# A forgetting-attention and FFN kernel on one core: q and k loaded per pair of heads and copied across partitions by ScalarE and VectorE

## The chip, the cores and the metric

The kernel runs on one core of a Trainium2 chip. The metric is the time of one execution on the device in microseconds; lower is better. Besides its memories a core has TensorE (PE; its weight loads are the rows PEld), VectorE (DVE), ScalarE (ACT), GpSimd (POOL) and SyncE (SP), which in this kernel issues all DMA transfers. Each engine works through its own queue in order; an instruction that waits holds up everything behind it on that engine.

## What is computed

```
scores = q k^T / 8 ;  cum = cumsum(log(clip(f, 1e-4, 1)))
scores = where(causal, -1e9, scores + cum[i] - cum[j])
attn   = softmax(scores)                     # 8 batches, 8 heads, S = 576, D = 64
x      = (attn v), heads side by side        # 4608 tokens x 512
h      = x w_in ; g = max(0.01 h, h) ; out = g w_out      # 512 -> 2048 -> 512, float32
```

## The kernel before, in words

Everything that needs full accuracy is split into a high part (`fp32r`, a float32 rounded for TensorE) and the low rest, and multiplied in two or three products. There are two kinds of work, and they run interleaved.

*Heads.* 64 heads, 8 to a batch, in two forms: in batches 0, 1 and 2 the first 256 queries are done in early steps ahead of the loop, so that only queries from 256 on are left there (24 heads, 320 columns of q); the other 40 heads are whole (576 columns). For head `t` the loop at L639 holds four kinds of step:

- `load(t)` (L215): q and k of one head come into `qraw` and `kraw`. Each is 64 rows (D) by 576, and each is loaded twice, into the lower and the upper 64 partitions (L223, four transfers). Both tiles have a single buffer. For the first head of a pair it also fetches v of both heads into `vm` (L227, L228).
- `split(t)` (L327): makes the operands of two products of 128 rows. The first is `s1` by `m1`: `m1` is the high part of k in both halves, `s1` the low part of q in the lower half and the high part in the upper half. The second is `s2` by `m2`: the upper half is the high part of q against the low part of k; in the lower half rows 0 to 3 hold the decay and ones, the others zeros. ScalarE makes the high parts (L337, L338, 128 partitions by 576), GpSimd the low ones by subtraction (L342, L343, through the helper at L133), and a transfer copies the high part of q from `s1` into `s2` (L339). Two small transfers bring the decay's rows (L340, L341). `s1` and `m1` have two buffers, `s2` and `m2` are four fixed tiles, a and b for even and odd heads. At last v is split into `vs` (L346, L347).
- `scores(t, i)` (L349): for each of up to five chunks of queries the two products (L362); VectorE adds the causal triangle `tri` and takes the extreme (L367); ScalarE takes the exponential and its sum (L373).
- `transposes`, `values`, `inverse`, `normalise` of the head before, `t - 1`: TensorE turns the chunks (L412), ScalarE and VectorE split the result into `ph` and `pl` (L424, L426); products with `vs` follow (L451), and ScalarE and VectorE add the two halves into `x` (L458 through the small tile `y`, L459). Once per pair `inverse` takes the reciprocals (L469, L470), turns them (`rt`, L472), writes them out (`rows`, L478) and reads them back across partitions (`rb`, `rbr`, L482); `normalise` multiplies (L494) and writes `xd` to memory (L497).

*FFN.* Groups of 256 tokens. `fetch_group` reads a group back from `xd` as `xs` (L508), `split_group` splits it (VectorE at L513, GpSimd), and the products `h` (L541) and `o` (L574) follow, with `g`, `gh`, `gl` between them (ScalarE L548, VectorE L551, GpSimd L553). A generator yields the FFN in small quanta, and `fill(step)` puts some of them between the steps of the heads, so that TensorE has something to do while the heads' chains run.

*What sets the order.* The text of the kernel gives each instruction its priority, and a planner (the scheduler of the tile framework) lays out every engine's queue from it: an instruction is put in line when, by the planner's own estimates of durations, what it needs is ready and its buffer is free. So a queue need not follow the order of the text, and work of a head can stand a step ahead of its place in the text. On the chip the queues then keep the planner's order, whatever really comes first.

Of the kernel before, what the change touches and what calls it, by code (L numbers as in the profile page):

```python
# [8 lines left out]
F32 = mybir.dt.float32  # L9
# [4 lines left out]
ALU = mybir.AluOpType  # L14

P = 128
# [21 lines left out]
def forgetting_attention_ffn(ctx, tc, qT, kT, v4, vr, f, w_in, w_out, out):  # L38
# [6 lines left out]
    nc = tc.nc  # L45
# [168 lines left out]

    def load(t):  # L215

        s, c0, c1 = tasks[t]
        h = state[t] = {}
        a, n = c0 * P, S
        for name, src, lo in (("q", qT, a), ("k", kT, 0)):  # L220
            x = h[name] = one.tile([P, S], F32, tag=f"{name}raw", name=f"{name}raw_{t}")
            for o in range(2):
                nc.sync.dma_start(x[o * D:(o + 1) * D, lo:n], src[s][:, lo:n])  # L223
        if s % 2 == 0:
            g = s // 2
            vm = fixed["vm"]
            nc.sync.dma_start(vm[:, :, :NFULL], v4[g])  # L227
            nc.sync.dma_start(vm[:REST, :, NFULL], vr[g])  # L228
            pairs[s // 2, c0] = {}
# [97 lines left out]
    def split(t):  # L327


        s, c0, c1 = tasks[t]  # L330
        h = state[t]
        a, n = c0 * P, S
        x = "ab"[t % 2]
        s1 = h["s1"] = one.tile([P, S], F32R, tag="s1", name=f"s1_{t}", bufs=2)
        m1 = h["m1"] = one.tile([P, S], F32R, tag="m1", name=f"m1_{t}", bufs=2)
        s2, m2 = h["s2"], h["m2"] = fixed["s2" + x], fixed["m2" + x]
        nc.scalar.copy(s1[:, a:n], h["q"][:, a:n])  # L337
        nc.scalar.copy(m1[:, :n], h["k"][:, :n])  # L338
        nc.sync.dma_start(s2[D:, a:n].bitcast(F32), s1[D:, a:n].bitcast(F32))  # L339
        nc.sync.dma_start(s2[2:4, a:n].bitcast(F32), dec_q[s][:, a:n])  # L340
        nc.sync.dma_start(m2[:2, :n].bitcast(F32), dec_k[s][:, :n])  # L341
        minus(s1[:D, a:n], h["q"][:D, a:n], s1[:D, a:n].bitcast(F32))  # L342
        minus(m2[D:, :n], h["k"][D:, :n], m1[D:, :n].bitcast(F32))  # L343
        o = s % 2
        vs, vm = fixed["vs"][:, o], fixed["vm"][:, o]
        nc.scalar.copy(vs[:, :, :D], vm)  # L346
        minus(vs[:, :, D:], vm, vs[:, :, :D].bitcast(F32))  # L347

    def scores(t, i):  # L349
# [9 lines left out]
        for x, (a, b) in enumerate(parts):  # L359
# [6 lines left out]
            at = TRI - P + m - n + a  # L366
# [96 lines left out]
    def inverse(t):  # L463
# [9 lines left out]
        main = one.tile([P, NFULL * P], F32, tag="part0", name=f"rb_{t}")  # L473
        rest = one.tile([P, 2 * P], F32, tag="part1", name=f"rbr_{t}")
        flat = rest[:2 * NCH, P:]
# [4 lines left out]
        for y, lo, hi in ((main[:, a:], a + P, NCH * P), (rest[:, :REST], a, a + REST)):  # L480
            for o in range(2):
                nc.sync.dma_start(  # L482
                    y[o * D:(o + 1) * D], to[o:o + 1, lo:hi].broadcast_to([D, hi - lo])
                )
        pairs[s // 2, c0]["r"] = main, rest

    def normalise(t):

        s, c0, c1 = tasks[t]
        pair = pairs[s // 2, c0]  # L490
        x, (main, rest) = pair["x"], pair["r"]
        a, n = c0 * P, S
        for y, lo, hi in ((main[:, a:], a + REST, n), (rest[:, :REST], a, a + REST)):
            nc.vector.tensor_tensor(x[:, lo:hi], x[:, lo:hi], y, op=ALU.mult)  # L494
        b, hp = s // HPB, (s % HPB) // 2
        at = place[b, a]
        nc.sync.dma_start(xd[hp * P:(hp + 1) * P, at:at + n - a], x[:, a:n])  # L497
# [117 lines left out]
    TRI = S  # L615
# [21 lines left out]
    load(0)  # L637
    split(0)
    for t in range(nt + 1):  # L639
        heads[0] = t < nt  # L640
        if t + 1 < nt:
            load(t + 1)
# [6 lines left out]
        for i in range(5):  # L649
# [4 lines left out]
            if i == 1 and t and tasks[t - 1][0] % 2:  # L654
                inverse(t - 1)
            fill(step)
# [47 lines left out]
```

## Time and profile before

| | |
|---|---|
| median of 3 runs | 1221.16 us (1220.94 to 1221.28) |
| the profiled execution | 1219.51 us |
| its span, first to last instruction | 1217.7 us |
| TensorE's mean granted clock | 0.947 |
| DMA, share of 16 engines | 29.7% |
| HBM read, written | 82.62 MB, 18.58 MB |

How to read the lines. In the list of groups a line stands for all instructions of one line of the kernel, one engine and one shape: `out<-in`, shapes, count, then busy time and mean duration in ns, then the idle time of the engine just before them and what ended it. In the view of waits a row says which engine's line waited for what: us in total, times, longest. The timeline gives start and duration in us, and in brackets the idle time before and what ended it; rows `SPq` are transfers being issued, not moved. In the chain of waits a DMA row is the time from its issue to its landing. In the table by windows the columns are the stretch, its length, the busy us of PE, PEld, DVE, ACT and POOL with their instructions, the granted clock, the DMA share and GB/s. Matmuls overlap and their ends are modelled, so a busy TensorE is not one at its peak; its idle time is what counts here.

### The profile page before, as it was taken

How to read it: one execution, taken by the hardware profiler on the slowest of the kernel's cores; microseconds unless marked ns; L12 is line 12 of the kernel's file. 1: busy time of each engine (PE TensorE's matmuls, PEld its weight loads, DVE VectorE, ACT ScalarE, POOL GpSimd, SP SyncE). 2: the span in 40 equal slices, each digit the busy share in tenths (PEclk: the TensorE clock that was granted, in tenths of full speed). 3: DMA queues.
4: the chain of work that ended last, by engine and by line, in shares of the span. 5: the costliest groups of instructions: out<-in, count | busy, mean ns of one | idle time of the engine just before them, and what ended most of it. 6: DMA issues, size and time to landing. Idle time of an engine off the chain costs nothing.

```text
span 1217.7 us, 22171 instructions
## 1 busy us (share of the span) xinstructions
PE 1193.7 (98%) x7876; PEld 1077.6 (88%) x7876; DVE 612.8 (50%) x1682; ACT 631.0 (52%) x1631; POOL 429.3 (35%) x347
## 2 busy tenths in 40 slices
PE   8899999989999999999999999999999999999998
PEld 6678899988889999999999999999999998999997
DVE  7889556656645455544554434344444334553111
ACT  6876456667755565555544545455444444552111
POOL 1000354445444344444434434343344334432000
PEclk9899999989999999999999999999999999999999
DMA  6555234344342233323322223231223122211000
GB/s 208 167 193 171 81 96 119 89 133 112 100 125 80 81 97 107 97 71 96 97 89 60 89 69 95 74 94 54 79 75 92 58 75 75 75 54 46 18 18 19
DMA packets 81103, 110.54 MB, mean 91 GB/s; under 512 B 19616, under 2 KB 50704, under 8 KB 80992
## 3 DMA queue, kind: packets, MB, share of 16 engines
q1 hardware_dynamic: 80992, 109.11, 29.7%
q8 instruction: 63, 1.03, 0.4%
q14 instruction: 48, 0.39, 0.1%
HBM read 82.62 MB, written 18.58 MB: 83 GB/s over the span
## 4 chain that ended last, share of the span: by engine, by line
PE 86%; DMA 5%; DVE 4%; ACT 3%; issue 1%; POOL 0%; SPq 0%; ACTq 0%; DVEq 0%; POOLq 0%
PE h L541 31%; PE o L574 31%; PE av L451 8%; PE tr L412 7%; PE sc L362 7%; DMA xs<-xd 2%; DMA xd<-x 1%; PE sce L256 1%; DVE fixed_z L367 1%; DMA qraw<-in_qT 1%; PE ave L298 1%; DVE pl L426 1%; ACT fixed_z L373 0%; DMA wraw<-in_w_out 0%; DMA wraw<-in_w_in 0%
## 5 line engine op out<-in xcount | busy, mean ns | idle before, releaser
L541 PE MATMUL h<-xh,win_h 128*128 128x256 f32 x1152 | 331.3, 288 | 0.3 <-ACT xh L306 0.3
L541 PE MATMUL h<-xh,win_l 128*128 128x256 f32 x1152 | 327.6, 284 | 0.0
L541 PE MATMUL h<-xs,win_h 128*128 128x256 f32 x1024 | 289.3, 282 | 0.0
L553 POOL TENSOR_TENSOR gl<-g,gh 128x512 fp32r<-128x512 f32 x111 | 143.3, 1291 | 323.9 <-DVE gh L551 315.5
L574 PE MATMUL o<-wout_h,gh 128*128 128x512 f32 x576 | 233.2, 405 | 0.0
L574 PE MATMUL o<-wout_l,gh 128*128 128x512 f32 x576 | 227.0, 394 | 0.0
L574 PE MATMUL o<-wout_h,gl 128*128 128x512 f32 x576 | 225.6, 393 | 0.0
L541 PEld LDWEIGHTS h<-xh,win_h 128*128 128x128 f32 x1152 | 219.9, 191 | 3.5 <-ACT xh L306 0.8
L541 PEld LDWEIGHTS h<-xh,win_l 128*128 128x128 f32 x1152 | 220.3, 191 | 0.8 <-issue 0.7
L373 ACT ACTIVATE fixed_z<-fixed_z,max 128x192 f32<-128x192 f32 (+3 forms) x272 | 161.0, 592 | 105.1 <-DVE max L367 101.2
L367 DVE CUSTOM_DVE_ANT_0 fixed_z<-sc,tri 128x192 f32<-128x192 f32 (+3 forms) x272 | 121.8, 450 | 164.9 <-PE sc L362 162.9
L424 ACT CAST ph<-tr 128x64 fp32r<-128x64 f32 (+3 forms) x360 | 127.0, 374 | 147.2 <-PE tr L412 108.3
L548 ACT ACTIVATE g<-h 128x512 f32<-128x512 f32 x144 | 85.9, 597 | 217.4 <-PE h L541 214.7
L541 PEld LDWEIGHTS h<-xs,win_h 128*128 128x128 f32 x1024 | 195.3, 191 | 2.1
L426 DVE TENSOR_TENSOR pl<-tr,ph 128x64 fp32r<-128x64 f32 (+3 forms) x360 | 145.8, 422 | 76.2 <-ACT ph L424 75.3
L551 DVE CAST gh<-g 128x512 fp32r<-128x512 f32 x144 | 69.0, 479 | 193.9 <-ACT g L548 191.0
L412 PE MATMUL tr<-ident_r,fixed_z 128*128 128x128 f32 x888 | 146.8, 276 | 4.9 <-DVE x L459 2.7
L133 POOL TENSOR_TENSOR s<-qraw,s 64x576 fp32r<-64x576 f32 (+1 forms) x64 | 78.6, 1229 | 190.0 <-ACT s L337 185.3
L412 PEld LDWEIGHTS tr<-ident_r,fixed_z 128*128 128x128 f32 x888 | 109.0, 140 | 24.8 <-DVE x L459 2.9
L574 PEld LDWEIGHTS o<-wout_h,gl 128*128 128x128 f32 x576 | 108.4, 188 | 24.1 <-DVE maxe L269 0.4
L362 PE MATMUL sc<-m,s 128*128 128x288 f32 (+1 forms) x336 | 121.1, 365 | 3.6 <-DVE max L367 3.5
L574 PEld LDWEIGHTS o<-wout_h,gh 128*128 128x128 f32 x576 | 109.0, 189 | 15.7 <-issue 0.4
(107 smaller groups left out, 1687.6 us busy)
## 6 DMA issues: line engine op xcount, KB each, us to landing
kraw<-in_kT SPq DMA_DIRECT2D x128, 144.0 KB
qraw<-in_qT SPq DMA_DIRECT2D x80, 144.0 KB
wraw<-in_w_in SPq DMA_DIRECT2D x16, 512.0 KB
wraw<-in_w_out SPq DMA_DIRECT2D x16, 512.0 KB
fixed_vm<-in_v SPq DMA_DIRECT2D x32, 256.0 KB
xs<-xd SPq DMA_DIRECT2D x16, 512.0 KB
out<-ost SPq DMA_DIRECT2D x28, 256.0 KB
xd<-x SPq DMA_DIRECT2D x20, 288.0 KB
```

Source lines behind the costliest of these rows:

```text
L133: nc.gpsimd.tensor_tensor(out, a, b, op=ALU.subtract)
L362: nc.tensor.matmul(ps[:, :b - a], h["s" + w][:, q:q + P], h["m" + w][:, a:b], start=y == 0, stop=y == 1,)
L367: nc.vector.tensor_tensor_reduce(out=z[:, a:b], in0=ps[:m, :b - a], in1=tri[:m, at:at + b - a], scale=-SCALE, scalar=3.0e38 if x == 0 else ...
L373: nc.scalar.activation(z, z, AF.Exp, bias=h["max"][:m, last:last + 1], scale=-1.0, accum_out=fixed["sum" + "ab"[s // 2 % 2]][:m, i, s % 2: ...
L412: nc.tensor.transpose(ps[:, a:a + P], fixed[f"z{x}"][:, j * P:(j + 1) * P], ident)
L424: nc.scalar.copy(o, src)
L426: nc.vector.tensor_tensor(o, src, hi.bitcast(F32), op=ALU.subtract)
L451: nc.tensor.matmul(ps[:, a - lo:hi - lo], fixed["vs"][:, odd, j, :], h[w][:, at:at + hi - a], start=(n == 0), stop=(n == len(steps) - 1),)
L541: nc.tensor.matmul(ph[:, e, :], w[:, c, fs], xx[:, c, :], start=(c == 0 and x == 0), stop=(c == NCC - 1 and x == 2),)
L548: nc.scalar.activation(g, ph, AF.Prelu, alpha=0.01)
L553: eng.tensor_tensor(gl, g, gh.bitcast(F32), op=ALU.subtract)
L574: nc.tensor.matmul(acc[k], gg[:, e, ts], w[:, e, :], start=(fc_ == 2 * p0 and x == 0), stop=(fc_ == 2 * p1 - 1 and x == 2),)
```

## The change

- A pair's q and k are loaded at once, 128 partitions by 576: the even head in the lower half, the odd one in the upper half. `load` is called once per pair, with v, and its place in the text is behind the third chunk of the step before an even head (`i == 2`), no longer the head of every step.
- `split` reads the head's own half. The halves that a head's second copy supplied are made by copying across partitions: ScalarE and VectorE each cast k into one half of `m1`; ScalarE casts q into the half beside it and VectorE into the other (`near`, `far`). The transfer from `s1` to `s2` is gone. GpSimd's two subtractions write upper halves, reading the head's own half.
- The low part of q now lies in the upper half of `s1` and the high part in the lower one.
- The decay's two transfers move from `split` to `load_decay(t + 1)`, at the head of the step.
- `inverse` reads the row back with two broadcasts into one tile of 640 columns, where it were four into two tiles; the small tile that it writes out lies in buffer `y` now. `normalise` multiplies the same two stretches.
- `tri` is 128 columns narrower, and `scores` computes the place in it accordingly.

```diff
     state = {}
     pairs = {}
 
+    raw = {}
+
     def load(t):
+
+        s, c0, c1 = tasks[t]
+        g, a = s // 2, c0 * P
+        for name, src, lo in (("q", qT, a), ("k", kT, 0)):
+            x = raw[name] = one.tile([P, S], F32, tag=f"{name}raw", name=f"{name}raw_{t}")
+            nc.sync.dma_start(x[:, lo:], src[s:s + 2, :, lo:].rearrange("s d n -> (s d) n"))
+        vm = fixed["vm"]
+        nc.sync.dma_start(vm[:, :, :NFULL], v4[g])
+        nc.sync.dma_start(vm[:REST, :, NFULL], vr[g])
+        pairs[g, c0] = {}
+
+    def load_decay(t):
 
         s, c0, c1 = tasks[t]
         h = state[t] = {}
-        a, n = c0 * P, S
-        for name, src, lo in (("q", qT, a), ("k", kT, 0)):
-            x = h[name] = one.tile([P, S], F32, tag=f"{name}raw", name=f"{name}raw_{t}")
-            for o in range(2):
-                nc.sync.dma_start(x[o * D:(o + 1) * D, lo:n], src[s][:, lo:n])
-        if s % 2 == 0:
-            g = s // 2
-            vm = fixed["vm"]
-            nc.sync.dma_start(vm[:, :, :NFULL], v4[g])
-            nc.sync.dma_start(vm[:REST, :, NFULL], vr[g])
-            pairs[s // 2, c0] = {}
+        a, x = c0 * P, "ab"[t % 2]
+        s2, m2 = h["s2"], h["m2"] = fixed["s2" + x], fixed["m2" + x]
+        nc.sync.dma_start(s2[2:4, a:].bitcast(F32), dec_q[s][:, a:])
+        nc.sync.dma_start(m2[:2].bitcast(F32), dec_k[s])
...
@@ split
-        s2, m2 = h["s2"], h["m2"] = fixed["s2" + x], fixed["m2" + x]
-        nc.scalar.copy(s1[:, a:n], h["q"][:, a:n])
-        nc.scalar.copy(m1[:, :n], h["k"][:, :n])
-        nc.sync.dma_start(s2[D:, a:n].bitcast(F32), s1[D:, a:n].bitcast(F32))
-        nc.sync.dma_start(s2[2:4, a:n].bitcast(F32), dec_q[s][:, a:n])
-        nc.sync.dma_start(m2[:2, :n].bitcast(F32), dec_k[s][:, :n])
-        minus(s1[:D, a:n], h["q"][:D, a:n], s1[:D, a:n].bitcast(F32))
-        minus(m2[D:, :n], h["k"][D:, :n], m1[D:, :n].bitcast(F32))
-        o = s % 2
+        s2, m2 = h["s2"], h["m2"]
+        low, up = slice(0, D), slice(D, P)
+        mine, other = (low, up) if o == 0 else (up, low)
+        k, q = raw["k"][mine], raw["q"][mine, a:]
+        near, far = (s1[low, a:], s2[up, a:]) if o == 0 else (s2[up, a:], s1[low, a:])
+        nc.scalar.copy(m1[mine], k)
+        nc.vector.tensor_copy(m1[other], k)
+        nc.scalar.copy(near, q)
+        nc.vector.tensor_copy(far, q)
+        minus(m2[up], k, m1[mine].bitcast(F32))
+        minus(s1[up, a:], q, near.bitcast(F32))
...
@@ scores
-            at = TRI - P + m - n + a
+            at = TRI - n + m - P + a if b == n else 0
...
@@ inverse
-        main = one.tile([P, NFULL * P], F32, tag="part0", name=f"rb_{t}")
-        rest = one.tile([P, 2 * P], F32, tag="part1", name=f"rbr_{t}")
-        flat = rest[:2 * NCH, P:]
+        main = one.tile([P, NCH * P], F32, tag="part0", name=f"rb_{t}")
+        flat = one.tile([P, P], F32, tag="y", name=f"rt_{t}")[:2 * NCH]
...
-        for y, lo, hi in ((main[:, a:], a + P, NCH * P), (rest[:, :REST], a, a + REST)):
-            for o in range(2):
-                nc.sync.dma_start(
-                    y[o * D:(o + 1) * D], to[o:o + 1, lo:hi].broadcast_to([D, hi - lo])
-                )
+        for o in range(2):
+            nc.sync.dma_start(
+                main[o * D:(o + 1) * D, a:], to[o:o + 1, a:].broadcast_to([D, NCH * P - a])
+            )
...
@@ normalise
-        for y, lo, hi in ((main[:, a:], a + REST, n), (rest[:, :REST], a, a + REST)):
-            nc.vector.tensor_tensor(x[:, lo:hi], x[:, lo:hi], y, op=ALU.mult)
+        for lo, hi, at in ((a + REST, n, a + P), (a, a + REST, a)):
+            nc.vector.tensor_tensor(
+                x[:, lo:hi], x[:, lo:hi], main[:, at:at + hi - lo], op=ALU.mult
+            )
...
-    TRI = S
+    TRI = S - P
...
     load(0)
+    load_decay(0)
     split(0)
     for t in range(nt + 1):
         heads[0] = t < nt
         if t + 1 < nt:
-            load(t + 1)
+            load_decay(t + 1)
...
             if i == 1 and t and tasks[t - 1][0] % 2:
                 inverse(t - 1)
+            if i == 2 and t + 1 < nt and tasks[t + 1][0] % 2 == 0:
+                load(t + 1)
             fill(step)
```

More of the change, by code (lines that the diff above doesn't have):

```diff
@@ L331, in split @@
         h = state[t]
-        a, n = c0 * P, S
-        x = "ab"[t % 2]
+        a, o = c0 * P, s % 2
         s1 = h["s1"] = one.tile([P, S], F32R, tag="s1", name=f"s1_{t}", bufs=2)
         m1 = h["m1"] = one.tile([P, S], F32R, tag="m1", name=f"m1_{t}", bufs=2)
-        s2, m2 = h["s2"], h["m2"] = fixed["s2" + x], fixed["m2" + x]
-        nc.scalar.copy(s1[:, a:n], h["q"][:, a:n])
-        nc.scalar.copy(m1[:, :n], h["k"][:, :n])
-        nc.sync.dma_start(s2[D:, a:n].bitcast(F32), s1[D:, a:n].bitcast(F32))
-        nc.sync.dma_start(s2[2:4, a:n].bitcast(F32), dec_q[s][:, a:n])
-        nc.sync.dma_start(m2[:2, :n].bitcast(F32), dec_k[s][:, :n])
-        minus(s1[:D, a:n], h["q"][:D, a:n], s1[:D, a:n].bitcast(F32))
-        minus(m2[D:, :n], h["k"][D:, :n], m1[D:, :n].bitcast(F32))
-        o = s % 2
+        s2, m2 = h["s2"], h["m2"]
[9 more added lines that the diff above has]
+        minus(s1[up, a:], q, near.bitcast(F32))
         vs, vm = fixed["vs"][:, o], fixed["vm"][:, o]
@@ L479, in inverse @@
         a = c0 * P
-        for y, lo, hi in ((main[:, a:], a + P, NCH * P), (rest[:, :REST], a, a + REST)):
-            for o in range(2):
-                nc.sync.dma_start(
-                    y[o * D:(o + 1) * D], to[o:o + 1, lo:hi].broadcast_to([D, hi - lo])
-                )
-        pairs[s // 2, c0]["r"] = main, rest
+        for o in range(2):
+            nc.sync.dma_start(
+                main[o * D:(o + 1) * D, a:], to[o:o + 1, a:].broadcast_to([D, NCH * P - a])
+            )
+        pairs[s // 2, c0]["r"] = main
     def normalise(t):
@@ L490, in normalise @@
         pair = pairs[s // 2, c0]
-        x, (main, rest) = pair["x"], pair["r"]
+        x, main = pair["x"], pair["r"]
         a, n = c0 * P, S
-        for y, lo, hi in ((main[:, a:], a + REST, n), (rest[:, :REST], a, a + REST)):
-            nc.vector.tensor_tensor(x[:, lo:hi], x[:, lo:hi], y, op=ALU.mult)
+        for lo, hi, at in ((a + REST, n, a + P), (a, a + REST, a)):
+            nc.vector.tensor_tensor(
+                x[:, lo:hi], x[:, lo:hi], main[:, at:at + hi - lo], op=ALU.mult
+            )
         b, hp = s // HPB, (s % HPB) // 2
```

## The prediction, made before the changed kernel was run

> **What bounds the kernel.** I read the page's busy table first, then who waited for whom on TensorE, then a table by stage, then the timeline of the worst stage, engine by engine.
>
> ```profile
> span 1217.7 us, 22171 instructions
> PE 1193.7 (98%) x7876; PEld 1077.6 (88%) x7876; DVE 612.8 (50%) x1682; ACT 631.0 (52%) x1631; POOL 429.3 (35%) x347
> ```
>
> TensorE is busy for 1193.7 of 1217.7 us. The change leaves every matmul and transpose as it is, so TensorE's own work stays, and the time can move only through TensorE's idle time (24.0 us in all, the start and the tail included) and through its clock. The next view is TensorE's idle time by what ended it (total, times, longest):
>
> ```profile
> PE sce L256 <- DVE maxe L269: 5.1, 6, 2.7
> PE sc L362 <- DVE max L367: 3.5, 3, 2.0
> PE tr L412 <- DVE x L459: 2.7, 1, 2.7
> PE tr L412 <- DVE pl L426: 2.2, 4, 0.8
> PE rt L472 <- DVE pl L426: 2.0, 4, 0.5
> PE rt L472 <- DVE x L459: 0.6, 1, 0.6
> ```
>
> The first row lies in the early steps, which the change doesn't touch. The other five come to 11.0 us. That is all that could be won here, and every one of them is a wait for VectorE. By stage (us from the start; busy of PE, PEld, DVE, ACT, POOL; clock; DMA):
>
> ```profile
> 130.00:345.00 215.00, 207.52 (x1395) 188.86 (x1391) 124.51 (x373) 132.23 (x360) 97.82 (x84) 0.94 0.37 107
> 345.00:1100.00 755.00, 751.11 (x5058) 691.50 (x5059) 350.05 (x1032) 388.07 (x1018) 315.78 (x241) 0.95 0.28 81
> 251.00:255.00 4.00, 1.26 (x12) 1.06 (x10) 2.68 (x6) 2.68 (x6) 3.32 (x2) 0.95 0.26 74
> 255.00:259.00 4.00, 3.52 (x16) 2.83 (x15) 2.45 (x9) 2.29 (x10) 2.58 (x3) 0.57 0.27 75
> ```
>
> From 345 on TensorE idles 3.9 us in 755. From 130 to 345 it idles 7.5 us, 2.7 of them in one hole at 251 to 255, and right behind the hole the granted clock is 0.57 instead of 0.95 for 4 us: that stretch did (0.95-0.57)/0.95 x 4 = 1.6 us less than it could have. So this one hole costs about 4.3 us, and the question is what made it. VectorE there, then SyncE, which issues all transfers, ScalarE and TensorE:
>
> ```profile
> 246.74 0.45 DVE L367 CUSTOM_DVE_ANT_0 fixed_z<-sc,tri 128x288 f32<-128x288 f32 x1
> 250.83 0.69 DVE L513 CAST xh<-xs 128x1024 fp32r<-128x1024 f32 x1 [3.63 <-DMA xs<-xd]
> 252.96 1.03 DVE L469 TENSOR_SCALAR r<-fixed_suma 128x10 f32<-128x10 f32 x1 [1.00 <-ACT fixed_z L373]
> 254.15 0.56 DVE L459 TENSOR_TENSOR x<-av,y 64x448 f32<-64x448 f32 x1
> ```
> ```profile
> 238.89 0.47 SPq L223 DMA_DIRECT2D qraw<-in_qT  x1
> 241.42 0.58 SPq L227 DMA_DIRECT2D fixed_vm<-in_v  x1
> 242.10 0.55 SPq L497 DMA_DIRECT2D xd<-x  x1
> 243.31 0.61 SPq L223 DMA_DIRECT2D qraw<-in_qT  x1
> 243.97 0.59 SPq L223 DMA_DIRECT2D kraw<-in_kT  x1
> 245.29 0.39 SPq L508 DMA_DIRECT2D xs<-xd  x1
> 245.73 1.06 SPq L223 DMA_DIRECT2D kraw<-in_kT  x1
> 247.32 0.26 SPq L341 DMA_DIRECT2D fixed_m2b<-dec_k  x1
> ```
> ```profile
> 251.07 0.68 ACT L338 CAST m<-kraw 128x576 fp32r<-128x576 f32 x1 [2.26 <-DMA kraw<-in_kT]
> ```
> ```profile
> 254.77 0.44 PE L412 MATMUL tr<-ident_r,fixed_z 128*128 128x128 f32 x2 [2.73 <-DVE x L459]
> ```
>
> VectorE runs in order. It stands from 247.2 until 250.83 for `xs` (the next FFN group), and behind it wait the scores of a head, the inverse and the addition `x` at 254.15, whose end lets TensorE go on. ScalarE stands for a late half of k meanwhile. The `xs` read is issued at 245.29 and lands 5.5 us later. Around it SyncE issued v, `xd`, half of q and both halves of k, one after the other, 4.4 us after the first half of q; the decays that follow go to `m2b`, so this is the load of an odd head.
>
> **The change, part by part.** *Loads.* Per pair of heads, q and k take 2 transfers instead of 8, the copy of q's upper half into `s2` goes (2), and the inverse's broadcasts go from 4 to 2. With v (2), the decays (4), `rows` and `xd`, a pair takes 12 issues instead of 22. No TensorE instruction waits for a transfer as such in the rows above, so what this is worth is what it does for the two late transfers of the hole and others like it. How long `xs` takes with less traffic beside it, the chain of waits shows at four other places:
>
> ```profile
> 339.46 3.68 DMA xs<-xd
> 594.76 3.38 DMA xs<-xd
> 897.31 3.38 DMA xs<-xd
> 1019.25 4.69 DMA xs<-xd
> ```
>
> An odd head now loads no q and k, and the hole lies where an odd head's were loading. So at 245.29 only v and `xd` remain beside `xs`, and I take 3.4 us instead of 5.5: VectorE goes on 2.1 us earlier. Everything behind it is shifted by that, since ScalarE's copy of k no longer waits (row 251.07) and `r` stands behind GpSimd's split of the same group, which shifts too. The hole shrinks from 2.7 to 0.6 us: -2.1. With so short a hole I expect no slow stretch behind it: -1.6. Both hang on one thing, and neither is certain. Bounds: 0, if something else is late in place of `xs`, and -4.3.
>
> ```profile
> 344.91 0.40 PE L362 MATMUL sc<-m,s 128*128 128x288 f32 x1 [1.97 <-DVE max L367]
> ```
>
> At 1019 `xs` took 4.69; down to 3.4 it could give 1.3, but the scores' three waits of 3.5 us have their longest at 344.91, which leaves 1.5 for two others: I take -0.7 (0 to -1.3). At 339.46, ahead of the longest, `xs` took 3.68, near its shortest: -0.3 (0 to -0.5). Sum of what the transfers give back: 2.1 + 1.6 + 0.7 + 0.3 = 4.7 us.
>
> *Copies.* ScalarE's two casts for a head stay two, over half the partitions. Half the partitions is no saving where the length per partition is the same, so I take 0 either way (677 ns each); GpSimd's two subtractions stay at 64 partitions by 576, one of them now reading lower partitions and writing upper ones. What that crossing costs no row shows for GpSimd; ScalarE's copy at L458 crosses too, from PSUM. I take 0 (a gain has no reason, and if the 1450 ns doubled, GpSimd at 35% would still hide it).
>
> ```profile
> L338 ACT CAST m<-kraw 128x576 fp32r<-128x576 f32 x64 | 43.3, 677 | 5.8 <-DMA kraw<-in_kT 5.7
> L133 POOL TENSOR_TENSOR fixed_m2b<-kraw,m 64x576 fp32r<-64x576 f32 x32 | 46.4, 1450 | 3.1 <-ACT m L338 0.9
> L551 DVE CAST gh<-g 128x512 fp32r<-128x512 f32 x144 | 69.0, 479 | 193.9 <-ACT g L548 191.0 <-PE ave L299 0.9 <-PE o L574 0.2
> L513 DVE CAST xh<-xs 128x1024 fp32r<-128x1024 f32 x16 | 13.4, 836 | 33.0 <-DMA xs<-xd 33.0
> ```
>
> VectorE gets two new casts per head. From 479 ns at 512 and 836 at 1024 a cast of 576 takes 479 + 64 x 0.70 = 524 ns, so 1.05 us per head, and some 55 to 65 us over 64 heads (24 of them have q at 320), on an engine that every wait of TensorE names. From 345 on this is covered: of the 33.0 us that VectorE stood for `xs`, the waits for transfers of 3.38 us (rows 594.76 and 897.31) stopped TensorE for no more than about 0.8 (row `PE tr` behind `pl`), so 1 us more in a step is hidden there; if that cover is gone, 48 heads at 0.1 us would be 5. From 130 to 345 it is not so covered. Eight inverses, one per pair, fall there, the first and the last of them these:
>
> ```profile
> 172.56 0.28 PE L472 MATMUL rt<-ident_r,r 128*10 128x128 f32 x1
> 325.69 0.27 PE L472 MATMUL rt<-ident_r,r 128*10 128x128 f32 x1 [0.51 <-DVE pl L426]
> ```
>
> That is 14 heads in 153 us, 11 us each. VectorE worked 124.5 us there, and TensorE stood for it 2.7 + 2.0 + 2.0 + 0.6 = 7.3 us, 0.06 us for each us of work. Some 16 heads add 17 us of casts, and about 0.9 us each for one of two that falls behind GpSimd (below), 14 us: 31 x 0.06 = +1.8. Bounds: 0, if the casts fall into VectorE's waits, and 8 pairs x 0.9 = +7.2, if each pair's inverse waits for a blocked cast.
>
> *The rest.* The decays' transfers move to the head of a step. They still wait until the scores two heads back have read `s2` and `m2`; they are small, and nothing in the new split has to wait behind them that waited for less before. The pair's load, four issues of about 0.6 us (rows 241.42 to 243.97), moves in the text past `rows`, its broadcasts and a fetch of `xs`; only SyncE's queue is concerned, and a load can't start before the last reader of q and k is done, so I count nothing for the place. The new casts wait for that load on VectorE, with scores, `pl` and `x` queued behind them, where only ScalarE waited (5.8 us in the row of L338). With half the loads I expect at most 3 us of it, and by the 0.06 above 0.2 of that on TensorE: inside the rounding. The inverse's small tile now shares buffer `y`: ScalarE's copy at the end of the step must wait for a transfer begun in the second chunk of it, several us before. Nothing. `tri` is only smaller.
>
> Sum: -4.7 + 1.8 = -2.9 us. The profiled execution took 1219.51 us (span 1217.7 and 1.8 around it), the median of the runs is 1221.16, so it was 1.65 us quicker than the usual run. I expect 1216.6 for a profiled run like it, and 1218.3 for the median.
>
> **The rivals.** *The transfers were hidden anyway.* `xs` can't start before `xd` has landed (the chain goes from one to the other), and VectorE's order is set by the planner, not by when data come. If the planner, too, counts on an earlier `xs`, VectorE stops for it as long as before. For it: v and `xd` stay beside it. Against: 5.5 us is far over the 3.38 seen twice. The hole then stays, the casts cost their lower half: 1221.2 to 1222, say 1221.4.
>
> *VectorE held by GpSimd: slower.* The trace has one VectorE instruction in two lengths:
>
> ```profile
> 240.58 0.90 DVE L494 TENSOR_TENSOR x<-x,rbr 128x64 f32<-128x64 f32 x1
> 335.41 0.21 DVE L494 TENSOR_TENSOR x<-x,rbr 128x64 f32<-128x64 f32 x1
> 240.45 0.94 POOL L133 TENSOR_TENSOR fixed_vs<-fixed_vm,fixed_vs 128x320 fp32r<-128x320 f32 x1
> ```
>
> The long one ends as GpSimd's subtraction ends, at 241.4; so the 0.69 us more is waiting. The new casts are issued at the moment when GpSimd's subtractions of the same head start, 1.45 us each. If the second cast of each head is held in this way and the inverse of a pair stands behind it, TensorE waits some 0.9 us more at each of the eight inverses of the stage, +7.2. With half of the transfers' gain (-2.4) that is +4.8, so 1226.0; it decides when over half of the held casts lie ahead of an inverse. For it: the stage is dense and `rt` already waits at five pairs. Against: VectorE stands idle for ScalarE's exponential just ahead of the inverse (1.00 us in row 252.96), where the casts fit. The Trainium skill's page "SBUF — State Buffer" (Who interferes with whom) speaks against this change: it has a VectorE copy that uses two ports and a GpSimd instruction lock each other out for a whole instruction. By that rule both casts of a head can be held, or hold GpSimd; the trace agrees for the multiply with 0.90 against 0.21 us, and for a cast it is this rival.
>
> *A different order helps more.* The planner lays all queues out anew, and the wait of 2.0 us near 343 goes as well: -7, 1214.2.
>
> *The change does less than it says.* The queue's order is the planner's: the two halves of one q load stand 4.4 us apart. If it puts the pair's load behind v again, even heads wait as odd ones did. That ends in the first rival.
>
> **How the numbers follow.** Forecast 0.50, with a range of its own from 1215.7 to 1220.7; hidden (with the last) 0.25; held 0.20; another order 0.05. A measurement of this kernel can tell some 0.2%, 2.4 us, from no change: below 1218.7 is faster, above 1223.6 slower. Three quarters of the forecast's chance lies below 1218.7 (0.38), with the other order 0.43. Within 0.2%: the forecast's rest 0.12 and nearly all of the hidden case 0.23, 0.35. Slower: 0.22, the held case and a little of the hidden one. The range for 8 in 10 goes from 1214.0 to 1226.5: half of the held case, half of the better order and the forecast's thin ends are left out, not quite 2 in 10.
>
> **What would show it.** Right: no row of TensorE waiting 2.7 us near 250, no second stretch at half clock, ScalarE's waits for `kraw` gone, `xs` landing in about 3.4 us there, `PE rt` waits no longer than 1 us each. Wrong: a hole of over 2 us in the same stage behind another wait; casts of 1.2 us and more on VectorE with `rt` or `tr` waiting for them; GpSimd's subtractions much over 1.45 us; or more idle time of TensorE after 345 than 3.9 us.

## The result and the profile after

The changed kernel takes 1230.24 us (median of 4 runs, 1229.54 to 1232.99) where the kernel before took 1221.05 us beside it: ratio 1.0091, 95% interval 1.0066 to 1.0115. Measured once more it was 1.0102 (1.0081 to 1.0124). It is slower by about 1%: 9 us in the first measurement, 12.5 in the second. The forecast was 1218.3 us, the range ended at 1226.5: wrong in sign and in size.

The profiled execution took 1232.99 us. Its busy table:

```profile
span 1230.9 us, 21659 instructions
PE 1203.7 (98%) x7876; PEld 1081.3 (88%) x7876; DVE 750.1 (61%) x1810; ACT 635.7 (52%) x1631; POOL 442.2 (36%) x347
```

ScalarE does what it did (631.0 before). VectorE has 128 instructions more and works 137 us more, where I had reckoned with 55 to 65. GpSimd works 13 us more on as many instructions. TensorE's waits (total, times, longest) and the two stages, then the place of the hole in three slices of 4 us:

```profile
PE tr L420 <- DVE pl L434: 4.9, 6, 1.5
PE tr L420 <- DVE x L467: 3.8, 1, 3.8
PE sc L370 <- DVE max L375: 3.1, 3, 1.9
PE rt L480 <- DVE pl L434: 1.4, 3, 0.8
PE rt L480 <- DVE x L467: 1.3, 3, 0.4
```
```profile
130.00:345.00 215.00, 206.05 (x1362) 184.35 (x1362) 158.22 (x400) 133.69 (x356) 99.97 (x87) 0.99 0.22 69
345.00:1100.00 755.00, 747.70 (x5022) 687.17 (x5021) 450.52 (x1119) 389.91 (x1016) 326.45 (x241) 1.00 0.19 60
```
```profile
256.00:260.00 4.00, 2.11 (x18) 1.91 (x16) 3.97 (x5) 1.76 (x4) 3.32 (x3) 1.00 0.00 0
260.00:264.00 4.00, 2.07 (x12) 1.93 (x13) 3.04 (x10) 1.83 (x7) 1.30 (x2) 0.84 0.51 147
264.00:268.00 4.00, 4.00 (x18) 3.29 (x17) 1.69 (x8) 1.84 (x6) 0.58 (x1) 0.73 0.15 51
```

The hole is still there and longer, 3.8 us in place of 2.7, with VectorE busy all through it (3.97 of 4 us), and a stretch at a low granted clock still follows. From 345 on TensorE idles 7.3 us where it was 3.9. (The clock of 0.99 and 1.00 in the two stages against 0.94 and 0.95 is not the change's: later executions of the kernel before have means of 0.985 to 0.999 and take 1214.7 to 1226.8 us.)

Where is the time lost? The same matmuls can be timed in each trace from one mark to the next (us; the marks are named by their time in the kernel before, and from 172.6 on they are the inverse's transposes `rt`; the last two kernels are those of the third and fourth experiment):

| from, to | before | changed | changed, second trace | casts of both not held | far copies by transfer |
|---|---|---|---|---|---|
| 55.6, 160.0 | 104.5 | 107.1 | 107.5 | 106.7 | 104.1 |
| 160.0, 172.6 | 12.5 | 14.0 | 13.9 | 12.5 | 12.5 |
| 172.6, 355.2 | 182.7 | 189.2 | 190.4 | 183.9 | 180.5 |
| 355.2, 613.5 | 258.3 | 260.8 | 260.8 | 258.2 | 259.0 |
| 613.5, 1100.3 | 486.8 | 486.2 | 486.4 | 485.5 | 486.8 |

Most of the loss lies between 172.6 and 355.2, which is the stage that the prediction had priced: there TensorE idles 9.7 us instead of 7.5, and the clock is at half for 6.8 us instead of 3.4. Some 2.5 us follow up to 613, and none after that. The first row is another matter. All kernels of this study that have the new loads and casts on VectorE take 2.2 to 3.1 us longer there, held or not, the others without such casts at most 0.1; but the changed kernel has a single one of these casts before 138 us. What differs there is the planner's order: of the 7876 places in TensorE's queue 145 hold another product than before, nearly all of them between 69 and 133 us. (The first 55 us differ by up to 9 us between the traces, with no link to the change.)

The groups that answer to the forecast casts, and the line of k's cast by itself (shortest, median, longest, ns):

```profile
L348 DVE CAST m<-kraw 64x576 fp32r<-64x576 f32 x64 | 58.1, 908 | 2.2 <-PE sc L370 0.2
L350 DVE CAST s<-qraw 64x576 fp32r<-64x576 f32 x20 | 31.2, 1558 | 0.1
L350 DVE CAST fixed_s2a<-qraw 64x576 fp32r<-64x576 f32 x20 | 28.7, 1436 | 0.2
L133 POOL TENSOR_TENSOR s<-qraw,s 64x576 fp32r<-64x576 f32 x20 | 32.8, 1640 | 0.0
```
```profile
L348 DVE CAST m<-kraw x64: 453/1208/2348, 138.9 to 1086.8; 64x576 fp32r<-64x576 f32 x64
```

One instruction of one shape takes anything from 453 to 2348 ns. The shortest is its work (my estimate was 524); the rest is waiting inside the instruction, which the profile counts as busy. GpSimd's subtraction took 1426 ns in the kernel before. The hole shows what is waited for; VectorE, then GpSimd:

```profile
255.10 1.97 DVE L521 CAST xh<-xs 128x1024 fp32r<-128x1024 f32 x1 [1.81 <-DMA xs<-xd]
257.53 2.35 DVE L348 CAST m<-kraw 64x576 fp32r<-64x576 f32 x1
259.80 1.11 DVE L350 CAST s<-qraw 64x576 fp32r<-64x576 f32 x1
260.94 0.17 DVE L477 TENSOR_SCALAR r<-fixed_suma 128x10 f32<-128x10 f32 x1
261.28 0.56 DVE L467 TENSOR_TENSOR x<-av,y 64x448 f32<-64x448 f32 x1
```
```profile
253.68 1.44 POOL L133 TENSOR_TENSOR fixed_m2b<-kraw,m 64x576 fp32r<-64x576 f32 x1 [3.06 <-ACT m L347]
255.09 1.43 POOL L133 TENSOR_TENSOR s<-qraw,fixed_s2b 64x576 fp32r<-64x576 f32 x1
257.20 2.37 POOL L133 TENSOR_TENSOR xs<-xs,xh 128x1024 fp32r<-128x1024 f32 x1 [0.68 <-DVE xh L521]
259.52 1.07 POOL L133 TENSOR_TENSOR fixed_vs<-fixed_vm,fixed_vs 128x320 fp32r<-128x320 f32 x1
```

`xh` starts with GpSimd in the subtraction for `s` and ends 0.5 us behind its end; k's cast starts 0.3 us behind GpSimd's 2.37 us split of the FFN group and lasts as long; q's cast lasts about as long as the split of v. Each GpSimd instruction holds one VectorE instruction here. The forecast half of the hole did come true: VectorE stood 1.81 us for `xs` instead of 3.63. But 5.4 us of held casts stand where 0.69 us of `xh` and 1.03 of `r` stood.

### The profile page after: what moved, and what is told of

Its sections match the earlier page's. It is cut to its first block, busy times and chain, and to the rows that moved or that the text cites. A ratio compares the mean times of both kernels' runs of the same rounds, so it can differ in the third digit from the quotient of the medians.

```text
span 1230.9 us, 21659 instructions
## 1 busy us (share of the span) xinstructions
PE 1203.7 (98%) x7876; PEld 1081.3 (88%) x7876; DVE 750.1 (61%) x1810; ACT 635.7 (52%) x1631; POOL 442.2 (36%) x347
## 3 DMA queue, kind: packets, MB, share of 16 engines
q8 instruction: 63, 1.03, 0.3%
## 4 chain that ended last, share of the span: by engine, by line
PE 83%; DVE 8%; DMA 4%; ACT 2%; issue 2%; POOL 0%; SPq 0%; DVEq 0%; ACTq 0%; POOLq 0%
PE h L549 30%; PE o L582 29%; PE tr L420 7%; PE av L459 7%; PE sc L370 6%; DMA xs<-xd 2%; DMA xd<-x 2%; DVE fixed_z L375 1%; DVE m L348 1%; PE sce L263 1%; DVE pl L434 1%; PE ave L305 1%; DVE s L350 1%; PE warm L108 1%; PE sce L266 1%
## 5 line engine op out<-in xcount | busy, mean ns | idle before, releaser
L559 DVE CAST gh<-g 128x512 fp32r<-128x512 f32 x144 | 66.3, 460 | 168.5 <-ACT g L556 165.8
L582 PEld LDWEIGHTS o<-wout_l,gh 128*128 128x128 f32 x576 | 109.1, 189 | 14.6
```

Source lines behind the costliest of these rows:

```text
L559: nc.vector.tensor_copy(gh, g)
L582: nc.tensor.matmul(acc[k], gg[:, e, ts], w[:, e, :], start=(fc_ == 2 * p0 and x == 0), stop=(fc_ == 2 * p1 - 1 and x == 2),)
```

## The experiments

Two theories. *Held:* the casts' length is the loss, because GpSimd holds them; what is not held costs little. *Work:* any engine that gets 128 more instructions in the dense stage costs as much. A third question was where the transfers' gain had gone. The table collects what all runs gave, with 95% intervals; "stretch" is worked out from the timeline and explained under the eighth experiment. The kernels with a star have an extra small tile, `junk`, and with it a gain of about 0.0029 that has nothing to do with the casts: see the third experiment.

| kernel | ratio to before | VectorE busy, us | stretch, us |
|---|---|---|---|
| before | 1 | 612.8 | 2.16 |
| changed (second measurement) | 1.0102 (1.0081 to 1.0124) | 750.6 | 3.20 |
| far copies on ScalarE | 1.0057 (1.0039 to 1.0075) | 609.0 | 2.96 |
| copies alone | 1.0102 (1.0082 to 1.0121) | 743.8 | 3.25 |
| changed, r not held * | 1.0052 (1.0036 to 1.0068) | 732.0 | 2.87 |
| changed, casts of k not held * | 1.0033 (1.0017 to 1.0049) | 717.3 | 2.73 |
| changed, casts of q not held * | 1.0027 (1.0011 to 1.0042) | 705.4 | 2.36 |
| changed, casts of both not held * | 1.0018 (1.0004 to 1.0032) | 703.7 | 2.56 |
| changed, casts and r not held * | 1.0015 (0.9999 to 1.0032) | 688.1 | 2.28 |
| far copies by transfer | 0.9976 (0.9956 to 0.9996) | 612.1 | 2.19 |
| far copies by transfer, order undone | 0.9994 (0.9975 to 1.0013) | 611.9 | 2.18 |
| before, inverse's part alone | 0.9991 (0.9972 to 1.0010) | 613.9 | 2.16 |
| before, r not held * | 0.9966 (0.9946 to 0.9985) | 600.8 | 2.18 |
| far copies by transfer, r not held * | 0.9955 (0.9938 to 0.9972) | 602.3 | 2.10 |

**1. Far copies on ScalarE.** Changed kernel, with

```diff
-        nc.vector.tensor_copy(m1[other], k)
+        nc.scalar.copy(m1[other], k)
-        nc.vector.tensor_copy(far, q)
+        nc.scalar.copy(far, q)
```

> The changed kernel with the two far copies of each head on ScalarE instead of VectorE; loads and order as changed. Theory A (the casts on VectorE, held by GpSimd's subtractions in the dense stage, cost the 9 us): VectorE falls back to about 613 us busy, the hole near 255 falls under 1 us, time 1215 to 1222, with ScalarE's 1.35 us more per head costing at most 2. Theory B (the new loads and their order cost it): 1228 to 1232, as the changed kernel.

Measured 1226.50 us (1224.75 to 1230.29), above what was expected, though the hole near 255 is down to 0.9 us as expected. VectorE is back at 609.0 us and ScalarE rises from 635.7 to 718.0. Half of the loss stays, so ScalarE is not free either. Where it goes, VectorE's waits show (kernel before, then this one):

```profile
DVE x L459 <- ACT y L458: 72.4, 72, 2.2
DVE r L469 <- ACT fixed_z L373: 30.0, 31, 1.9
```
```profile
DVE x L467 <- ACT y L466: 90.3, 77, 2.8
DVE r L477 <- ACT fixed_z L381: 48.1, 30, 2.0
```

ScalarE's casts stand in its queue ahead of the exponential and of `y`, and VectorE waits 18 us more for each of the two. The theory of work is right in part.

**2. Copies alone.** The kernel before, with each of ScalarE's casts halved:

```diff
-        nc.scalar.copy(s1[:, a:n], h["q"][:, a:n])
-        nc.scalar.copy(m1[:, :n], h["k"][:, :n])
+        nc.scalar.copy(s1[:D, a:n], h["q"][:D, a:n])
+        nc.vector.tensor_copy(s1[D:, a:n], h["q"][D:, a:n])
+        nc.scalar.copy(m1[D:, :n], h["k"][D:, :n])
+        nc.vector.tensor_copy(m1[:D, :n], h["k"][:D, :n])
```

> The kernel before, with its two casts per head divided between ScalarE (one half of the partitions) and VectorE (the other half); loads, order and transfers as before. Theory A: VectorE gets the same two casts per head, 0.9 to 2.4 us each when held, and the time goes to 1227 to 1233. Theory B: no more than 1 us from the kernel before, 1220 to 1222.

Measured 1232.65 us (1228.93 to 1235.52), as much as the whole change, without a transfer changed and without a copy across partitions:

```profile
L340 DVE CAST m<-kraw 64x576 fp32r<-64x576 f32 x64 | 91.2, 1426 | 1.5
```

The casts on VectorE are enough for the loss. Across partitions or not makes no difference that these runs show: the shortest cast of 64x576 is 444 ns here and 453 in the changed kernel.

**3. Casts not held.** Changed kernel, the same copies written as a `tensor_scalar` with an accumulator:

```diff
-        nc.vector.tensor_copy(m1[other], k)
+        nc.vector.tensor_scalar(m1[other], k, 1.0, 0.0, op0=ALU.mult, op1=ALU.add, accum_out=junk[other, 0:1])
```

and likewise for `far`. The order of instructions on every engine stays that of the changed kernel.

> The changed kernel with each VectorE cast written as a tensor_scalar (times 1, plus 0) that also writes out its accumulator, which by the Trainium skill's page on SBUF can't take the port shared with GpSimd. Theory A in its narrow form (being held is what costs): each cast 0.65 to 0.8 us whatever GpSimd does, against 0.91 (k) and 1.06 to 1.56 (q) now; VectorE 1.5 us per head instead of 2.3; time 1219 to 1225. Theory A in its wide form (VectorE's work as such): 1226 to 1230. Theory B: 1228 to 1232.

Measured 1221.46 us (1219.61 to 1228.67), within what the narrow form expected.

```profile
L349 DVE TENSOR_SCALAR_CACHE_REDUCE m<-kraw 64x576 fp32r<-64x576 f32 x64 | 47.8, 747 | 2.2 <-PE sc L371 0.2
L133 POOL TENSOR_TENSOR s<-qraw,s 64x576 fp32r<-64x576 f32 x20 | 28.5, 1424 | 0.0
```

All 64 casts of k now take 746 to 752 ns, whatever GpSimd does, and GpSimd's subtraction is back at 1424. Each cast is slower than a free one by 294 ns, and still the kernel gets 0.84% back (1.0102 less 1.0018), about 10 us. Not all of that is the hold. The form needs the tile `junk` for its accumulators, and in all seven kernels that have this tile, in none of the others, the matmuls of the FFN run at another rhythm. It is there from 1105 to 1195 us, too, where no accumulating instruction runs any more (the kernel before, then the kernel before with `r` not held, of the seventh experiment):

```profile
L541 PE MATMUL h<-xh,win_h 128*128 128x256 f32 x126 | 35.7, 283 | 0.0
L574 PE MATMUL o<-wout_l,gh 128*128 128x512 f32 x64 | 25.1, 392 | 0.0
```
```profile
L542 PE MATMUL h<-xh,win_h 128*128 128x256 f32 x130 | 36.3, 279 | 0.0
L575 PE MATMUL o<-wout_l,gh 128*128 128x512 f32 x64 | 25.3, 396 | 0.0
```

After 1100 us the median distance from the start of one `h` matmul to the next is 117 ns instead of 120, from one `o` to the next 232 instead of 227. Summed over the kernel's successive pairs this is 7.1 to 7.3 us won and 3.6 to 3.8 lost: a net gain of about 3.5 us, 0.29%, in each of the seven, and at most 0.3 us either way in the others. What the tile changes for the matmuls, no run shows; no kernel with the tile alone was measured.

Without this the casts that aren't held give back about 0.55% (0.3 to 0.8), 6.7 us of the 12.5. So the hold is shown, and it is about half of the whole loss. In the traces it is nearly all of the part where the casts stand: from 160 to 613 us the changed kernel takes 464.0 and 465.1 us, this one 454.6 (some 1.3 of the difference being the rhythm), the kernel before 453.4. And it works in both directions. The Trainium skill's page "SBUF — State Buffer" (Who interferes with whom) has casts contend with GpSimd by an exclusive lock, and excepts a `tensor_scalar` that also writes out its accumulator: the trace agrees in both, 453 to 2348 ns against 746 to 752.

**4. Far copies by transfer.** Changed kernel, no cast on VectorE:

```diff
-        nc.vector.tensor_copy(m1[other], k)
+        nc.sync.dma_start(m1[other].bitcast(F32), m1[mine].bitcast(F32))
-        nc.vector.tensor_copy(far, q)
+        nc.sync.dma_start(far.bitcast(F32), near.bitcast(F32))
```

> The changed kernel with the two far copies of each head as transfers within SBUF (the kernel before had one such, 2 now); no casts on VectorE, none more on ScalarE. Theory A: 1215 to 1222, the hole near 255 under 1.5 us. Theory B: 1228 to 1232.

Measured 1216.20 us (1213.73 to 1223.83): 0.9976 (0.9956 to 0.9996), just faster than before. What the change does besides the casts gives 2.9 us (0.5 to 5.4); the casts that are not held cost 5.1 us on top of it (1.0018 less 0.9976), 8.6 without the gain by rhythm, and 2.2 to 3.1 of these belong to the other order in the early steps. The hole stays at 2.3 us where under 1.5 was expected, for VectorE is still held in it:

```profile
245.89 1.30 DVE L521 CAST xh<-xs 128x1024 fp32r<-128x1024 f32 x1 [2.47 <-DMA xs<-xd]
248.62 1.10 DVE L477 TENSOR_SCALAR r<-fixed_suma 128x10 f32<-128x10 f32 x1 [1.00 <-ACT fixed_z L381]
```

`r` only adds a constant to 128x10 numbers, and it takes 1.1 us. That led to the next one.

**5. Far copies by transfer, r not held.** As 4, and in `inverse`

```diff
-        nc.vector.tensor_scalar(r, sums, 1.0e-9, None, op0=ALU.add)
+        nc.vector.tensor_scalar(r, sums, 1.0, 1.0e-9, op0=ALU.mult, op1=ALU.add, accum_out=junk)
```

> As the kernel with the far copies by transfer (1216.2 us), and the sum that opens the inverse (r) written as a tensor_scalar with an accumulator, the form that GpSimd did not hold in the casts. In that kernel r was held up to 1.1 us by GpSimd behind the late xs. Theory (a held VectorE instruction ahead of the inverse costs TensorE what it waits): r takes 0.2 to 0.6 us everywhere, and the time falls by 0 to 2 us, to about 1215. Rival (r is held only where something else is late anyway, xs or the exponential): no change, within 0.7 us of the kernel without it.

Measured 1212.75 us (1209.75 to 1216.11), 0.9955 of before, 5.5 us: the fastest kernel of the study. Against the fourth that is 2.6 us, no more than the rhythm that comes with `junk` (3.5 us), so the time shows no gain from `r` itself. What the trace shows is the hole:

```profile
249.10 0.17 DVE L478 TENSOR_SCALAR_CACHE_REDUCE r<-fixed_suma 128x10 f32<-128x10 f32 x1 [1.00 <-ACT fixed_z L382]
```
```profile
PE tr L421 <- DVE x L468: 0.2, 1, 0.2
```

The hole is 0.2 us, and the granted clock stays at 1.00 from 246 to 260. This is the hole as I had forecast it (0.6 us, no slow stretch): in these traces it needed the transfers' gain and a free `r` together (2.3 us with the first alone, 1.5 with the second alone).

**6. Order undone.** As 4, with the pair's load at the head of the step and the decays' transfers ahead of the split:

```diff
-            load_decay(t + 1)
+        if t + 1 < nt and tasks[t + 1][0] % 2 == 0:
+            load(t + 1)
...
-            if i == 2 and t + 1 < nt and tasks[t + 1][0] % 2 == 0:
-                load(t + 1)
...
+            load_decay(t + 1)
```

> As the kernel with the far copies by transfer, but the pair's load stands at the head of the step again and the decays' two transfers at the end of it, just ahead of the split: the order of the transfers in the text as before the change, with the smaller number of them. If the 3.5 us by which the far copies by transfer beat the kernel before come from the number of transfers, the time stays at 1215 to 1217.5. If they come from the new order, it goes back to that of the kernel before, 1219 to 1220. If the load at the head of the step puts its four issues ahead of xs and xd, xs at about 250 lands later than in the moved order, and the hole there is over 2.3 us.

Measured 1216.82 us beside 1217.98, 0.9994 (0.9975 to 1.0013). The interval covers both answers, that of 4 and that of before. The hole did not grow (2.1 us; `xs` took 3.52). What the order is worth stays open: the two ratios differ by 2.2 us, less than the noise of the two measurements together.

**7. The inverse's part alone, and `r` alone in the kernel before.** The first is the kernel before with these parts of the change (in `scores`, `inverse`, `normalise`), the second the kernel before with the edit of 5.

```diff
-            at = TRI - P + m - n + a
+            at = TRI - n + m - P + a if b == n else 0
...
-        main = one.tile([P, NFULL * P], F32, tag="part0", name=f"rb_{t}")
-        rest = one.tile([P, 2 * P], F32, tag="part1", name=f"rbr_{t}")
+        main = one.tile([P, NCH * P], F32, tag="part0", name=f"rb_{t}")
...
+                main[o * D:(o + 1) * D, a:], to[o:o + 1, a:].broadcast_to([D, NCH * P - a])
```

> The kernel before with only the inverse changed: two broadcasts into one tile in place of four into two, its small tile in the buffer y, the narrower triangle; q and k loaded as before. Theory (the gain of the far copies by transfer comes from the loads): no change, within 1 us of the kernel before. Rival (the gain comes from the inverse's side): 2 to 4 us faster than before, near 1216.

> The kernel before with only the sum that opens the inverse (r) as a tensor_scalar with an accumulator, which GpSimd does not hold. Theory that held VectorE instructions cost TensorE time already before the change: 0 to 2 us faster than before, TensorE's waits for rt and tr behind VectorE shorter. Rival (covered by other waits): within 0.7 us.

The first took 1216.96 us, 0.9991 (0.9972 to 1.0010): no difference that can be told. The second took 1214.73 us, 0.9966 (0.9946 to 0.9985), 4.1 us less, and the mean of `r`, 32 times in the kernel, fell from 584 to 164 ns. But 3.5 of these 4.1 us are the rhythm of the matmuls that comes with `junk`; the 0.6 left is what the rival expected. That a held `r` cost time before the change is not shown. Against this kernel the changes of 5 bring nothing that can be told apart (0.9955 and 0.9966, measured beside each other).

**8. One kind of held instruction set free at a time.** Changed kernel; only k's casts, only `r`, both casts and `r`, and only q's casts in the other form (the edits of 3 and 5, one or two at a time), and the changed kernel itself again.

> The changed kernel with only the 64 casts of k as tensor_scalar with an accumulator; the casts of q stay as they were and can be held. With both kinds not held the time fell by 8.8 us against the changed kernel. Theory (what counts is how long a cast is held, whichever it is): the k casts were held 64 x (908 - 453) = 29 us in sum, the 40 whole q casts 40 x (1497 - 453) = 42 us, so the k casts give back 29/71 of it, 2.5 to 4.5 us: 1225 to 1228 beside a kernel before of 1219.5. Rival (the k cast comes first and the q cast of the same head simply takes over its waiting): 0 to 1 us, and the q casts are then held longer than 1.5 us on the mean.

> The changed kernel with only the sum that opens the inverse (r) as tensor_scalar with an accumulator; all casts as they were. In the kernel before this alone gave 3.2 us. Theory (each held instruction ahead of the inverse costs by itself): 2 to 4 us less than the changed kernel, 1225 to 1228 beside a kernel before of 1219.5. Rival (the casts in front of it take the hold of the same GpSimd instruction, so r is free anyway where it matters, as at 260.94 where it took 0.17 us): 0 to 1 us.

> The changed kernel with the casts of q and k and the sum that opens the inverse (r) all as tensor_scalar with an accumulator. With the casts alone it took 1221.5 us beside a kernel before of 1219.7. Theory: 2 to 4 us less, 1217.5 to 1219.5 beside 1219.7, no slower than the kernel before, and 3 to 6 us over the kernel with the far copies by transfer and r free (0.9955 of before), since the casts' own work stays on VectorE. Rival (r is hidden once the casts are not held): 1221 to 1222.

> The changed kernel itself once more, unaltered, as the base for the kernels that differ from it in one instruction: its first comparison had four runs a side and an interval of 0.5%. Copies alone (1.0102) less the rest (0.9976) adds up to 1.008; the kernels with one kind of instruction not held give 1.0033 and 1.0052. If the hold of the casts is worth about 7 us, the ratio is 1.007 to 1.009; if it was overrated by the first comparison, 1.005 to 1.006, and the hold of r then gave nothing in the kernel where only r was freed.

> The changed kernel with only the 64 casts of q as tensor_scalar with an accumulator; those of k can be held. With only those of k not held it took 1.0033 of the kernel before, with both 1.0018. Theory (k and q wait for the same GpSimd instructions; whichever can be held takes the wait): the k casts are then held longer than 908 ns on the mean, and the time stays near the changed kernel, 1.006 to 1.009. Rival (each cast's hold costs by itself): the q casts, held more in sum, give back as much as the k casts did, about 1.003.

The changed kernel came out at 1.0102, above both expectations. k alone gives back 0.69% (1.0102 less 1.0033), q alone 0.75%, both 0.84%, `r` alone 0.50%, and `r` on top of both 0.03%, nothing, as the rival had it. Less the rhythm of `junk` these are 4.9 us for k, 5.6 for q, 6.7 for both and 2.6 for `r`, each with some 3 us of noise either way. So for k the first theory (2.5 to 4.5 us) was a little low, for q the one with each hold by itself fits, and `r` came out as expected. But k and q don't add up: either kind alone gives back most of what both do. Two things in the timeline show why. First, a hold passes on. In the hole with only k's casts free, `r` takes it:

```profile
252.68 0.75 DVE L349 TENSOR_SCALAR_CACHE_REDUCE m<-kraw 64x576 fp32r<-64x576 f32 x1
253.36 0.45 DVE L351 CAST s<-qraw 64x576 fp32r<-64x576 f32 x1
253.84 2.22 DVE L478 TENSOR_SCALAR r<-fixed_suma 128x10 f32<-128x10 f32 x1
```

Second, there is a cover of limited length. In each head VectorE reads out the last chunk's extreme and later waits for ScalarE's `y` before it can add `x`. In the kernel before, then in the changed one at the same head (VectorE, then GpSimd, then the chain of waits behind it, then VectorE and TensorE):

```profile
454.80 0.08 DVE L367 DVE_READ_ACCUMULATOR2_ANT max<- 128x1 f32 x1
456.37 0.63 DVE L459 TENSOR_TENSOR x<-av,y 64x448 f32<-64x448 f32 x1 [1.49 <-ACT y L458]
```
```profile
465.17 0.08 DVE L375 DVE_READ_ACCUMULATOR2_ANT max<- 128x1 f32 x1
465.28 1.23 DVE L348 CAST m<-kraw 64x576 fp32r<-64x576 f32 x1
466.43 1.68 DVE L350 CAST fixed_s2a<-qraw 64x576 fp32r<-64x576 f32 x1
468.14 0.63 DVE L467 TENSOR_TENSOR x<-av,y 64x448 f32<-64x448 f32 x1
```
```profile
464.76 1.43 POOL L133 TENSOR_TENSOR fixed_m2a<-kraw,m 64x576 fp32r<-64x576 f32 x1 [1.36 <-ACT m L347]
466.15 1.64 POOL L133 TENSOR_TENSOR s<-qraw,s 64x576 fp32r<-64x576 f32 x1
```
```profile
471.60 3.47 DMA xd<-x
475.08 3.39 DMA xs<-xd
```
```profile
478.50 0.69 DVE L521 CAST xh<-xs 128x1024 fp32r<-128x1024 f32 x1 [4.77 <-DMA xs<-xd]
```
```profile
479.58 0.66 PE L420 MATMUL tr<-ident_r,fixed_z 128*128 128x128 f32 x4 [1.40 <-DVE pl L434]
```

The gap is 1.49 us. Two free casts of 453 ns would fit with room to spare. Two held ones, each ending 0.3 us behind the subtraction of GpSimd that had begun ahead of it, push `x` to 2.89 us behind the readout, 1.40 late. `normalise`, `xd` and `xs` follow one another, VectorE stops for `xs` with `pl` queued behind it (in the kernel before the planner had put that `pl` ahead of `xh`), and TensorE waits 1.40 us. In the kernel of the third experiment, with the same queues and no cast held, `x` comes 1.58 us behind the readout here, and TensorE waits 0.3. With one of the two free, the gap nearly holds; at the same head, q free, then k free:

```profile
457.18 1.23 DVE L349 CAST m<-kraw 64x576 fp32r<-64x576 f32 x1
459.19 0.63 DVE L468 TENSOR_TENSOR x<-av,y 64x448 f32<-64x448 f32 x1
```
```profile
459.22 0.55 DVE L351 CAST fixed_s2a<-qraw 64x576 fp32r<-64x576 f32 x1
459.99 0.63 DVE L468 TENSOR_TENSOR x<-av,y 64x448 f32<-64x448 f32 x1 [0.22 <-ACT y L467]
```

`x` comes 2.05 and 1.48 us behind the readout. The column "stretch" is this distance, the mean of the last 32 whole heads; in every second head `r` stands in it as well, so it is 1.49 to 3.66 us in the kernel before. Among the kernels with casts on VectorE the time rises with it. But a late `x` is not enough: from 613 us on the stretch is as long (mean 3.15 us, 2.19 before), and no time is lost there. The heads follow each other at about 19 us there, at 16 before; that TensorE then has enough other work until `xs` comes is how I read it, and no run tests it. Behind 355 us only two waits of TensorE grew by a microsecond or more: this one and one at 613.57 (0.54 before, 1.54 now). The share of each single hold isn't settled.

## Why the prediction was wrong, by its steps

*What bounds the kernel.* Right: TensorE's work stayed, every wait in the quoted rows names VectorE.

*VectorE's casts, +1.8 us: the step that failed.* Their length was not what failed: the 31 us of casts and holds that I priced for the stage came out, the 32 casts between 172.6 and 355.2 us took 31.4. (Nearly every cast of q and 35 of the 64 of k were held, not one in two; over the whole kernel the casts came to 144 us, where I had 55 to 65 without any hold.) What failed is the price, 0.06 us of TensorE's waiting for each us of VectorE's work. Against the far copies by transfer, the same change without casts on VectorE, that stage takes 8.7 and 9.9 us more in the two traces of the changed kernel: about 0.3 us for each us, five times the price, and over my upper bound of 7.2. The 0.06 is a mean over work that fits into VectorE's waits. The casts do not stand in those waits but ahead of `x` and `r`, where the room was 1.49 us and two held casts take 2.8; and behind the longer holes the clock was at half for longer (6.8 and 10.2 us in the stage against 3.4). The form that is not held, 22.8 us of casts in the same stage, cost 3.4 us there, about 4 without the rhythm.

*"From 345 on this is covered": 0.* It failed in part. I took VectorE's long waits for `xs` as the room in which a cast is free. The casts stand in front of `x`, whose lateness makes the next `xs` late: at 478.50 VectorE had waited 4.77 us for it, and TensorE 1.40. The idle time of TensorE from 345 on went from 3.9 to 7.3 us, and the changed kernel loses 2.5 us between 355 and 613. From 613 on, where `x` is as late, nothing is lost: there the cover held.

*What was not in the sum.* The 2.2 to 3.1 us of the early steps. "The planner lays all queues out anew" was in the prediction as a chance to win; in the early steps the new order cost time, with hardly a cast there.

*The hole, -2.1 and -1.6.* The mechanism was right and did not show. VectorE's wait for `xs` fell by 1.8 us (forecast 2.1); `xs` took 4.2 us, not 3.4. The held `xh`, k and q took its place, and the stretch at a low clock (0.84, 0.73) stayed. Without the casts the hole is 2.3 us, with `r` free as well 0.2. My row 252.96 showed `r` taking 1.03 us; I read that as work, and it was a hold (164 ns free).

*The transfers' gain in all, -4.7.* The rest of the change, with two transfers in place of the casts, is worth -2.9 us (-5.4 to -0.5). Mis-sized, if at all, and of the right sign. With the casts in, even this was lost: copies alone cost as much as the whole change.

*ScalarE's casts at 0, the inverse and the rest at 0.* Right for ScalarE (631.0 to 635.7 us) and for the inverse (0.9991); its waits for `kraw` at the hole are gone. *GpSimd's subtractions at 0.* The crossing of partitions is free (1424 ns where nothing holds it), but VectorE held them in turn: 1426 to 1640 ns.

*The rivals.* "VectorE held by GpSimd: slower" was the one, with 0.20. Its mechanism is shown by the third experiment. Its price for the stage, 8 inverses by 0.9 us, +7.2, was near the 8.7 and 9.9 us measured; its 1226.0 was too low for what it left out, the early steps' order and the 1.8 us that the casts cost between 355 and 613 against the far copies by transfer. Of what would show it wrong, three signs came: a hole over 2 us, casts of 1.2 us and more with `tr` waiting, more idle time after 345.

## What to carry to other kernels

Before work goes to an engine that waits a lot, find the gap that it will stand in, measure it (here 1.49 us), and set the longest duration against it that the shape can have while its neighbour works, not the shortest. A mean price of a microsecond, worked out over work that fits, doesn't hold for work that overfills a gap. Where an instruction of one shape shows two lengths, take the long one as the price and look for what runs beside it: here a form that was never held, slower by 294 ns when free, gave the kernel back about 0.55%.

And test a variant on a stretch that it can't have changed. The FFN's matmuls after 1100 us show that the kernels with a tile of a few columns more came with 0.29% of their own; without that look the free `r` in the kernel before passes for a gain of 0.34%.

## What the runs showed of the hardware beyond that

- A `tensor_scalar` over 128x10 numbers took 164 ns free and up to 2.22 us held. In the longest one GpSimd's split of the FFN group ran from 253.57 to 256.03 and `r` from 253.84 to 256.06: the hold cost what was left of GpSimd's instruction, however small the held one was.
- The same addition, with an accumulator, took 146 to 168 ns in all 32 places of each kernel that has it; its readout took another 83 ns.
- A stretch at half the granted clock for some us stood behind most holes of TensorE, but its place doesn't follow from the length of the one hole ahead of it: there was none behind holes of 2.12 us (order undone) and 2.20 us (casts of k not held), and one behind 2.29 us (casts of both not held) and 1.47 us (before, `r` not held). So in this study a shorter hole didn't always bring the clock back; what decides it stays open.
